# The last turns moved into their own slot, x^T's copies ahead of the weight conversion, and four weight pieces converted two slots later

## The chip, the core and the metric

The kernel runs on one NeuronCore of a Trainium2 chip. The time is that of one execution on the device, in microseconds (us). Five engines run their own instruction queues in order and meet at semaphores: PE (TensorE, the matmuls; its weight loads are listed apart as PEld), DVE (VectorE), ACT (ScalarE), POOL (GpSimd) and SP (SyncE, which only issues DMAs here). A number such as L401 is a line of the kernel before; where the kernel after is meant, its lines are some 1 to 18 further down.

## The reference

Attention with a threshold, and then a two-layer network with an exact GELU on the attention's output:

```python
scores = (1.0 / np.sqrt(64)) * np.matmul(q, k.transpose(0, 1, 3, 2))   # q, k, v: (8, 8, 576, 64)
thresh = np.max(scores, axis=-1, keepdims=True) - tau
scores = np.where(scores >= thresh, scores, -1e9)
scores = scores - np.max(scores, axis=-1, keepdims=True)
attn = np.exp(scores)
attn = attn / (np.sum(attn, axis=-1, keepdims=True) + 1e-09)
x = np.matmul(attn, v)           # then (B, H, S, D) -> (B*S, H*D): 4608 tokens x 512
h = x @ w_in                     # 512 -> 2048
g = 0.5 * h * (1.0 + erf(h / sqrt(2)))
out = g @ w_out                  # 2048 -> 512
```

The two weights arrive as float64 and have to be made float32 in the kernel; everything else is float32.

## The kernel before

**Slots.** The 64 heads are handled as 32 pairs `p` of heads, and the 576 queries of a pair in five chunks `i`: four of 128 (both heads, `e` = 0 and 1) and one of 64 + 64 (`i == NC`, both heads in one tile). One (p, i) is a slot `n`. One loop over `n` writes out, in program order, all that the engines do; nothing reorders it afterwards. The first batch element (pairs 0 to 3, the "early" pairs) has slots 0 to 19: slots 0 to 7 are chunks 0 and 1 of its pairs, slots 8 to 19 chunks 2, 3 and NC of each pair in turn, so that slot 19 is (3, NC). From slot 20 (`BATCH`) on the slots go pair by pair.

**A slot.** `scores` (PE, `sc`, L401) multiplies K^T and Q^T into two PSUM tiles, of which there are two in all, so the next slot's scores wait until this slot's are used up. `softmax_head`: DVE takes the negative row maximum (`nmx`, L413), POOL the threshold (`thr`, L416), ACT the exponential (`p`, L418). `softmax_tail`: DVE masks and sums (L434), which frees the score tile. For early pairs the probabilities are turned on PE one slot later (`turn_p_early`, `tr`, L347) and copied out of PSUM into `pT` by ACT (L354, L358, L363, L367). Slot 19's own turn is written out at the end of slot 20, and its copies are DVE's (`p == EARLY - 1`). From slot 20 on DVE turns the probabilities (L533) and SP regroups them by DMA. `weigh_v` multiplies V with the turned probabilities (PE, `xT`, L572) and ACT copies the result into the token block `xall` (L582). For an early pair's tokens from 256 on, that is put on a list (`due`) when its last turn is written out, and done in the next slot: slots 12, 15, 18 and 21.

**The network beside it.** `fill` puts matmuls of the two layers between the attention's: layer 1 `hT` (L664), whose results are kept as plain copies (L631) until slot 20, and layer 2 `o_ps` (L679), which needs them through the GELU. In slot 20 ACT switches its table, runs eight GELUs (L637) and switches back (L650). `fill` writes out a matmul only when the weight piece that it reads was written out before it as converted. `owed` is the work that fill may place in a slot; in slot 21 it places 0.4 of it and keeps the rest for slot 22.

**Conversion.** Each weight is loaded in 16 pieces of 128 x 512 float64, 32 in all, in this order: `w_in`, then `w_out` row block by row block, so that pieces 28 to 31 are blocks j = 12 to 15 of layer 2. A raw piece lies in a free slot of `xall` or in half of `turned_p`. Converting one takes four steps on three engines: `convert_first` on ACT (two activations, L199 and L200, into a `power` tile and the weight), `convert_second` on DVE (L207, L208), after which the next piece's load is issued by SP (L183), and `add_low_bits` on POOL (L219), the sum that finishes the piece. Of one slot's pieces the newest sum is written out ahead of the next slot's `thr`, the others behind both of its `thr`. The `power` tiles come from the pool `gp` of ten buffers, in which the GELU results lie too. `STEPS[n]` is the number of pieces that slot n converts, written out at the end of the slot; `convert_ahead` keeps one piece whose ACT part is done ahead. In slots 12, 15 and 18 (`hi == S` in `due`) the ACT part is written out ahead of `weigh_v` and its copies:

```python
        if early and n > START and any(hi == S for _, *_, hi in due):
            convert_ahead(STEPS[n] if n < BATCH - 1 else LATER)
```

`keep_busy` (L297) writes out matmuls on the identity whose result nobody reads; `BUSY` names the slots that have it. The rest of the kernel (the last ten token blocks, from L734 on) is not touched.

Of the kernel before, what the change touches and what calls it, by code (L numbers as in the profile page):

```python
# [9 lines left out]
U32 = mybir.dt.uint32  # L10
# [8 lines left out]
def kernel(  # L19
# [28 lines left out]
    nc = tc.nc  # L48
    ctx.enter_context(tc.manual_schedule())

    B, H, S, D = q.shape
    d_model, d_ff = moe_w_in.shape
    P = 128
    Q = 32
    HP = H // 2
    NP = B * HP
    EARLY = HP
# [44 lines left out]
    def x_slot(want=None):  # L102
        i = max(x_free) if want is None else want
        x_free.remove(i)
        return i
# [8 lines left out]
    def x_rows(i):  # L114
        return xall[:, i, :, :].rearrange("p c t -> p (c t)")
# [37 lines left out]
    pieces += [(w_out_sb[j][:, f:f + PIECE], moe_w_out[j * P:(j + 1) * P, f:f + PIECE])  # L153
               for j in range(N_DF) for f in range(0, d_model, PIECE)]
    wide = moe_w_in.dtype != FP32
    LATER = 2
    raws = []
    loaded = [0]
    converted = [0]

    def load_piece(eng=nc.sync):
        k = loaded[0]
        if k == len(pieces):
            return
        staged = k % 2 and k < len(pieces) - LATER
        if wide and not staged and not x_free:
            return
        dst, src = pieces[k]
        loaded[0] += 1
        if not wide:  # L170
            nc.sync.dma_start(dst, src)
            converted[0] += 1
            load_piece()
            return
        slot = []
        if staged:

            half, at = divmod(k // 2 % 4, 2)
            raw = pd[half].bitcast(U32)[:, at * 2 * PIECE:(at + 1) * 2 * PIECE]
        else:  # L180
            slot = [x_slot()]
            raw = x_rows(slot[0]).bitcast(U32)
        eng.dma_start(raw, src.bitcast(U32))  # L183
        raws.append((dst, raw, slot))

    ahead = []

# [34 lines left out]
    def convert_ahead(steps):  # L222

        while raws and len(ahead) <= steps:
            convert_first()

    def convert(steps):

        while steps > 0 and (ahead or raws):
            convert_ahead(1)  # L230
            convert_second()
            steps -= 1
# [104 lines left out]
    def turn_p_early(p, i):  # L337


        s = st[p]  # L340
        if i == 0 or (p < HP and i == 2):
            s["pT"] = [one.tile([P, KR, S], FP32, tag=f"pT{e}", name=f"pT{e}") for e in range(2)]
        w = s.pop(("p", i))
        n = 1 if i == NC else 2

        def turn(to, at):
            nc.tensor.transpose(to, w[:, at:at + P], ident)  # L347

        for e in range(n):
            tr = ps.tile([P, NC, P], FP32, tag="mm", name="tr")  # L350
            for c in range(NC):
                turn(tr[:, c, :], e * (S + TAIL) + c * P)
            if i < NC:
                nc.scalar.copy(s["pT"][e][:, 0:NC, i * P:(i + 1) * P], tr)  # L354
        if i == NC:
            copy = nc.vector.tensor_copy if p == EARLY - 1 else nc.scalar.copy
            for e in range(2):
                copy(s["pT"][e][:, 0:NC, MAIN:S], tr[:, :, e * TAIL:(e + 1) * TAIL])  # L358
        tails = s["pT"][0][:, NC, :]
        tr = ps.tile([P, NC, P], FP32, tag="mm", name="tr")  # L360
        turn(tr[:, 0, :], MAIN if i < NC else S - P)
        if i < NC:
            nc.scalar.copy(tails[:, i * P:(i + 1) * P], tr[:, 0, :])  # L363
            return
        for e in range(2):
            rows = slice(e * TAIL, (e + 1) * TAIL)
            copy(tails[rows, MAIN:S], tr[P - TAIL:P, 0, rows])  # L367

    def scale_q(p):
        t = st[p]["q"]  # L370
# [50 lines left out]
    def softmax_tail(p, i):  # L421

        s = st[p]
        sc, thr, w = s.pop(("sc", i)), s.pop(("thr", i)), s["p", i]
        n = len(sc)
        if p < EARLY and i < 2:
            pair = small.tile([P, 2], FP32, tag="den", name="den", bufs=2 * HP)
            den = [pair[:, e:e + 1] for e in range(n)]
        else:
            at = [e * NC + i if i < NC else 2 * NC for e in range(n)]  # L430
            den = [sums[p % 2][:, x:x + 1] for x in at]
        for e in range(n):
            row = w[:, e * S:(e + 1) * S].rearrange("p (h s) -> p h s", h=2)
            nc.vector.scalar_tensor_tensor(  # L434
                row, sc[e][:, :, 0:HALF], thr[:, e:e + 1], row, op0=ALU.is_ge, op1=ALU.mult, accum_out=den[e])
        if p < EARLY and i < 2:
            nc.gpsimd.tensor_scalar(pair[:, 0:n], pair[:, 0:n], 1e-9, None, op0=ALU.add)
            s["sum", i] = pair[:, 0:n]
        elif p < EARLY and i == NC:
            at = sums[p % 2][:, 0:2 * NC + 1]  # L440
            nc.gpsimd.tensor_scalar(at, at, 1e-9, None, op0=ALU.add)
# [112 lines left out]
            for e in (1, 0):  # L554
                nc.sync.dma_start(by_64(s["pT"][e])[:, 2 * a + h, :, :], turned_p[rows, e, h, :, :])

    def weigh_v(p, lo, hi):


        b, hp = divmod(p, HP)  # L560
        s = st[p]
        xT = ps.tile([P, 512], FP32, tag="mm", name="xT")
        for c in range(KR):
            for e in range(2):
                f = slice(e * D, (e + 1) * D)
                to = xT[f, 0:hi - lo]
                if p < EARLY:
                    rhs = s["pT"][0 if c == NC else e][:, c, lo:hi]
                else:
                    to = to.rearrange("p (g s) -> p g s", s=2 * Q)  # L570
                    rhs = by_64(s["pT"][e])[:, lo // (2 * Q):hi // (2 * Q), c, :]
                nc.tensor.matmul(  # L572
                    to, lhsT=s["v"][:, e, c, :], rhs=rhs, start=(c == 0), stop=(c == KR - 1))
        for n, o, at, size in in_blocks(b, lo, hi):
            if n not in x_blk:
                x_at[n] = x_slot(x_place(n))
                x_blk[n] = xall[:, x_at[n], :, :]
            to, x = x_blk[n][:, hp, o:o + size], xT[:, at - lo:at - lo + size]
            if p < EARLY and size == TOK:
                to = to.rearrange("q (p c) -> q c p", c=2)  # L580
                x = x.rearrange("q (c p) -> q c p", c=2)
            nc.scalar.copy(to, x)  # L582

    def weigh_half(p, c):

# [14 lines left out]
    def in_blocks(b, lo, hi):  # L600
        while lo < hi:
            n, o = divmod(b * S + lo, TOK)
            size = min(TOK - o, hi - lo)
            yield n, o, lo, size
            lo += size
# [513 lines left out]

    HALVED = (2, 3)  # L1120
    DIVIDE_LATE = {14: 0, 16: 1, 19: 2, 22: 3}
    STEPS = [0, 1, 1, 1, 1, 1, 2, 1, 2, 2, 2, 2, 3, 2, 2, 3, 2, 2, 2]
    BUSY = {1: 2, 6: 2, 8: 2, BATCH: 4}

    tokens = 0
    owed = 0.0
# [3 lines left out]
    for n in range(len(slots) + WEIGH + 1):  # L1130
# [17 lines left out]
        if n == BATCH:  # L1148
            gelus_held()
        table()  # L1150
        if early and n > START and any(hi == S for _, *_, hi in due):
            convert_ahead(STEPS[n] if n < BATCH - 1 else LATER)
        for args in due:
            if len(args) == 2:
                weigh_half(*args)
                if args[1]:
                    divide_early(args[0], 0, TOK)
                continue
            weigh_v(*args)
            if args[1] == 0:  # L1160
                divide_early(*args)
        due = []
        if n in DIVIDE_LATE:
            divide_late(DIVIDE_LATE[n])
        if p > EARLY and i == WEIGH:
# [10 lines left out]
            turn_p_early(*last)  # L1176
        if p < NP:
            softmax_tail(p, i)
        if p < NP and not early:
            turn_p(p, i)  # L1180
        if p < NP and not early:
            if i == 2:
                regroup(p, 1)
            if i > 2:
                regroup(p, i)
            if i == NC:
                divisors(p)
        if last and last[0] < EARLY and last[1] == NC:
            turn_p_early(*last)
        if p < 2 and i == 0:  # L1190
            for _ in range(2):
# [21 lines left out]
            scale_q(p + 1)  # L1213
        if p >= HP - 1 and i == 2 and p + 1 < NP:
            turn_qk(p + 1)
        convert(STEPS[n] if n < BATCH - 1 else len(pieces))
        if not early:
            lag[0] = 2 if p < NP else 0
            if n != BATCH:
                share = 0.4 if n == BATCH + 1 else 1.0  # L1220
                fill(owed * share, tokens)
                owed *= 1.0 - share
        if n in BUSY:
            keep_busy(BUSY[n])
        if last and last[0] < EARLY:
            if last[1] < 2 and last[0] in HALVED:
                due.append((last[0], last[1]))
            elif last[1] == 1:
                due.append((last[0], 0, TOK))
            if last[1] == NC:  # L1230
                due.append((last[0], TOK, S))
        if n == START - 1:
            tokens = TOK
        elif n == BATCH + 1:
            tokens = S
        elif p > EARLY and i == DIVIDE and p % HP == 0 or p == NP and i == WEIGH:
            tokens = p // HP * S
            leaving += [n for n in AWAY if n in x_blk and (n + 1) * TOK <= tokens]
        elif leaving and i < 2:
            put_away(leaving.pop(0))  # L1240
# [35 lines left out]
```

## Time and profile before

| what | value |
|---|---|
| median of three runs | 1333.94 us (1333.72 to 1334.61) |
| the profiled execution | 1333.98 us, of which its span 1332.1 us, 1.88 us around it |
| PE, DVE, ACT, POOL busy over the span | 99%, 78%, 45%, 48% |
| slots 0 to 19 | from 0 to 124.8 us; the scores of slot 20 start at 123.61 us |
| granted TensorE clock | 0.999 |

The profiler gives each instruction a start and a length. A row of the timeline merges equal instructions that follow each other: start, time from the first one's start to the last one's end, engine, line, operation, tiles, count, and in square brackets the idle time ahead of it with the instruction that ended the idle time. A float32 matmul counts as two records, so that x8 is four `sc` matmuls and x2 one of layer 2. The records of one engine overlap a little, so the step from start to start is what counts. A busy PE of 99% doesn't mean that PE never waits: a wait of a few tenths lies inside the records.

### The profile page before, as it was taken

How to read it: one execution, taken by the hardware profiler on the slowest of the kernel's cores; microseconds unless marked ns; L12 is line 12 of the kernel's file. 1: busy time of each engine (PE TensorE's matmuls, PEld its weight loads, DVE VectorE, ACT ScalarE, POOL GpSimd, SP SyncE). 2: the span in 40 equal slices, each digit the busy share in tenths (PEclk: the TensorE clock that was granted, in tenths of full speed). 3: DMA queues.
4: the chain of work that ended last, by engine and by line, in shares of the span. 5: the costliest groups of instructions: out<-in, count | busy, mean ns of one | idle time of the engine just before them, and what ended most of it. 6: DMA issues, size and time to landing. Idle time of an engine off the chain costs nothing.

```text
span 1332.1 us, 19898 instructions
## 1 busy us (share of the span) xinstructions
PE 1317.4 (99%) x6322; PEld 891.8 (67%) x6322; DVE 1041.0 (78%) x2003; ACT 603.8 (45%) x1025; POOL 635.2 (48%) x1058
## 2 busy tenths in 40 slices
PE   9999999999999999999999999999999999999998
PEld 6766466476476466466466556568788787877877
DVE  6887787788888888888888888783857698386674
ACT  7987357267367358348448438232211203211120
POOL 3555454545655655655655641236264403645530
PEclk9999999999999999999999999999999999999999
DMA  8463666776876887887797775400000130000003
GB/s 257 167 180 86 135 149 155 167 171 154 188 176 153 191 191 156 188 201 160 181 211 155 174 180 113 107 8 1 1 0 1 40 103 17 0 1 0 1 0 79
DMA packets 213687, 153.14 MB, mean 115 GB/s; under 512 B 117264, under 2 KB 196992, under 8 KB 213584
## 3 DMA queue, kind: packets, MB, share of 16 engines
q1 hardware_dynamic: 195440, 125.31, 40.6%
q0 software_dynamic: 17712, 26.26, 7.6%
q8 instruction: 52, 0.85, 0.3%
q14 instruction: 51, 0.42, 0.1%
q10 hardware_dynamic: 432, 0.30, 0.1%
HBM read 56.62 MB, written 12.58 MB: 52 GB/s over the span
## 4 chain that ended last, share of the span: by engine, by line
PE 91%; DVE 3%; ACT 2%; issue 1%; DMA 1%; POOL 1%; SPq 0%; DVEq 0%; POOLq 0%; ACTq 0%
PE bank L852 34%; PE o_ps L679 17%; PE hT L664 16%; PE sc L401 13%; PE xT L572 11%; DVE nmx L413 1%; DVE p L434 1%; ACT p L418 1%; PE tr L347 1%; DVE power L208 1%; DVE power L207 1%; ACT power L199 0%; DMA inv<-turned 0%; ACT w_out L200 0%; POOL thr L416 0%
## 5 line engine op out<-in xcount | busy, mean ns | idle before, releaser
L418 ACT ACTIVATE p<-sc,nmx 128x576 f32<-128x576 f32 x288 | 201.8, 737 | 282.3 <-DVE nmx L413 282.0
L434 DVE SCALAR_TENSOR_TENSOR p<-sc,thr,p 128x576 f32<-128x576 f32 x288 | 225.2, 815 | 72.9 <-ACT p L418 65.2
L416 POOL TENSOR_SCALAR thr<-nmx,tau_eff 128x1 f32<-128x1 f32 x288 | 83.9, 293 | 342.7 <-DVE nmx L413 340.8
L413 DVE TENSOR_REDUCE nmx<-sc 128x1 f32<-128x576 f32 x288 | 205.3, 749 | 46.9 <-PE sc L401 45.6
L664 PE MATMUL hT<-xall,w_in 128*128 128x256 f32 x1024 | 241.8, 386 | 0.0
L679 PE MATMUL o_ps<-w_out,g 128*128 128x512 f32 x512 | 236.8, 603 | 0.0
L664 PEld LDWEIGHTS hT<-xall,w_in 128*128 128x128 f32 x1024 | 189.4, 190 | 51.2 <-issue 24.5
L734 DVE TENSOR_TENSOR o<-o,bank 128x256 f32<-128x256 f32 (+1 forms) x242 | 99.9, 416 | 94.6 <-PE bank L852 89.6
L734 DVE TENSOR_TENSOR c<-c,bank 128x320 f32<-128x320 f32 x304 | 147.1, 487 | 33.8 <-PE bank L852 20.1
L679 PEld LDWEIGHTS o_ps<-w_out,g 128*128 128x128 f32 x512 | 93.1, 190 | 109.6 <-issue 106.5
L401 PE MATMUL sc<-kT,qT 64*128 64x288 f32 x960 | 159.8, 429 | 2.3 <-DVE p L434 1.6
L572 PE MATMUL xT<-pT,v 128*64 128x320 f32 (+1 forms) x1240 | 159.6, 409 | 0.7 <-DVE pT L358 0.5
L533 DVE STREAM_TRANSPOSE turned_p<-p 128x1152 f32<-128x1152 f32 x112 | 154.4, 1378 | 3.9
L401 PEld LDWEIGHTS sc<-kT,qT 64*128 64x128 f32 x960 | 91.4, 186 | 75.8 <-issue 60.4
L572 PEld LDWEIGHTS xT<-pT,v 128*64 128x64 f32 x1240 | 86.5, 137 | 71.5 <-issue 11.1
L852 PE MATMUL bank<-w_out,c 128*128 128x256 f32 (+1 forms) x484 | 120.5, 379 | 0.8 <-DVE o L734 0.8
L260 POOL DMA_DIRECT2D v<-in_v_dram x208 | 110.8, 536 | 3.7 <-issue 1.7
L852 PEld LDWEIGHTS bank<-w_out,c 128*128 128x128 f32 x484 | 90.3, 190 | 18.9 <-DVE o L734 3.2
L919 ACT ACTIVATE c<-c 128x320 f32<-128x320 f32 (+1 forms) x80 | 46.9, 624 | 114.6 <-DVE c L734 114.5
L852 PE MATMUL bank<-t_out,g 128*128 128x256 f32 (+1 forms) x324 | 82.4, 377 | 0.4 <-DVE o L734 0.4
L852 PE MATMUL bank<-t_out,c 128*128 128x256 f32 x320 | 82.8, 381 | 0.0
L734 POOL TENSOR_TENSOR c<-c,g 128x320 f32<-128x320 f32 (+1 forms) x40 | 50.5, 1271 | 67.5 <-DVE c L734 67.5
(186 smaller groups left out, 1753.7 us busy)
## 6 DMA issues: line engine op xcount, KB each, us to landing
pT<-turned_p SPq DMA_DIRECT2D x448, 160.0 KB, 3.6
pT<-pd_tail SPq DMA_DIRECT2D x112, 80.0 KB, 3.1
q<-in_q_dram POOLq DMA_DIRECT2D x104, 72.0 KB, 3.6
k<-in_k_dram POOLq DMA_DIRECT2D x104, 72.0 KB, 3.2
inv<-turned SPq DMA_DIRECT2D x54, 128.0 KB, 4.2
v<-in_v_dram POOLq DMA_DIRECT2D x156, 40.0 KB, 3.2
out_dram<-o SPq DMA_DIRECT2D x40, 128.0 KB, 2.4
xall<-in_moe_w_out_dram SPq DMA_DIRECT2D x9, 512.0 KB, 5.0
```

What stands on the lines that cost most here:

```text
L260: eng.dma_start(t[r:P:4, e, 0:n, :], rows[:, r * KR:r * KR + n, :])
L401: nc.tensor.matmul(sc[e][:, h, 0:HALF], lhsT=lhsT, rhs=s["kT"][rows, at:at + HALF], start=True, stop=True)
L413: nc.vector.tensor_reduce(nmx[:, e:e + 1], sc, axis=AXIS.XY, op=ALU.max, negate=True)
L416: nc.gpsimd.tensor_scalar(thr[:, e:e + 1], nmx[:, e:e + 1], -1.0, tau_eff, op0=ALU.mult, op1=ALU.subtract)
L418: nc.scalar.activation(w[:, e * S:(e + 1) * S].rearrange("p (h s) -> p h s", h=2), sc, AF.Exp, bias=nmx[:, e:e + 1], scale=1.0)
L434: nc.vector.scalar_tensor_tensor(row, sc[e][:, :, 0:HALF], thr[:, e:e + 1], row, op0=ALU.is_ge, op1=ALU.mult, accum_out=den[e])
L533: nc.vector.transpose(turned_p[:, :, i // 2, 0:NB, i % 2 * Q:(i % 2 + 1) * Q], w.rearrange("p (e b i) -> p e b i", e=2, i=Q))
L572: nc.tensor.matmul(to, lhsT=s["v"][:, e, c, :], rhs=rhs, start=(c == 0), stop=(c == KR - 1))
L664: nc.tensor.matmul(hT[:, j % 2, :], lhsT=w_in_sb[c][:, j * P:(j + 1) * P], rhs=x_blk[n][:, c, :], start=(c == 0), stop=(c == N_DM - 1))
L679: nc.tensor.matmul(o[:, 0:d_model], lhsT=g[j][:, m * P:(m + 1) * P], rhs=w_out_sb[j], start=(j == 0), stop=(j == N_DF - 1))
L734: eng.tensor_tensor(out, a, b, op=ALU.add)
L852: nc.tensor.matmul(to, lhsT=l, rhs=r, start=start and k == 0, stop=k == len(pairs) - 1, skip_group_check=not start)
```

## The change

- `LATER` is 4 in place of 2: raw pieces 28 to 31 are loaded into `xall`, none of them into `turned_p`. `load_piece` remembers a load that found no free slot (`wanted`) and issues it with a later one.
- `STEPS`: slots 2 and 4 convert no piece (one before), slots 6 and 18 one (two before), slots 21 and 22 two each (none before). Slot 18 leaves one piece with its ACT part done, so ACT does two pieces in slot 21 and one in slot 22.
- In slots 12, 15 and 18 the ACT part of the conversion is written out behind `weigh_v` and its copies.
- The turns of slot 19 are written out in slot 19, behind those of slot 18, and copied by ACT. Their `xT` comes in slot 20 (slot 21 before); its copies into `xall` are DVE's, behind slot 20's L533.
- `BUSY` loses its entry for slot 20: eight identity matmuls.
- In slot 21 `fill` places 0.75 of what is owed. In program order PE has eight layer-2 matmuls in slot 21 and three in slot 22, where it had four and seven; in slot 23 it has five (j = 11 to 15) both times.

```diff
-    LATER = 2
+    LATER = 4
...
     def load_piece(eng=nc.sync):
-        k = loaded[0]
-        if k == len(pieces):
-            return
-        staged = k % 2 and k < len(pieces) - LATER
-        if wide and not staged and not x_free:
-            return
...
+        wanted[0] += 1
+        while wanted[0] > 0 and loaded[0] < len(pieces):
+            k = loaded[0]
+            staged = k % 2 and k < len(pieces) - LATER
+            if wide and not staged and not x_free:
+                return
...
+            wanted[0] -= 1
...
         if i == NC:
-            copy = nc.vector.tensor_copy if p == EARLY - 1 else nc.scalar.copy
             for e in range(2):
-                copy(s["pT"][e][:, 0:NC, MAIN:S], tr[:, :, e * TAIL:(e + 1) * TAIL])
+                nc.scalar.copy(s["pT"][e][:, 0:NC, MAIN:S], tr[:, :, e * TAIL:(e + 1) * TAIL])
...
-    def weigh_v(p, lo, hi):
+    def weigh_v(p, lo, hi, copy=nc.scalar.copy):
...
+        if copy is None:
+            return xT
+        weighed(p, lo, hi, xT, copy)
+
+    def weighed(p, lo, hi, xT, copy):
...
-            nc.scalar.copy(to, x)
+            copy(to, x)
...
-    STEPS = [0, 1, 1, 1, 1, 1, 2, 1, 2, 2, 2, 2, 3, 2, 2, 3, 2, 2, 2]
-    BUSY = {1: 2, 6: 2, 8: 2, BATCH: 4}
+    STEPS = [0, 1, 0, 1, 0, 1, 1, 1, 2, 2, 2, 2, 3, 2, 2, 3, 2, 2, 1, 0, 0, 2, 2]
+    BUSY = {1: 2, 6: 2, 8: 2}
...
-        if early and n > START and any(hi == S for _, *_, hi in due):
-            convert_ahead(STEPS[n] if n < BATCH - 1 else LATER)
+        long = early and n > START and any(hi == S for _, *_, hi in due)
         for args in due:
...
+            if n == BATCH:
+                xT = weigh_v(*args, None)
+                continue
             weigh_v(*args)
...
+        if long:
+            convert_ahead(STEPS[n])
...
+        if n == BATCH - 1:
+            turn_p_early(p, i)
         if p < NP and not early:
             turn_p(p, i)
+        if n == BATCH:
+            weighed(EARLY - 1, TOK, S, xT, nc.vector.tensor_copy)
...
-        if last and last[0] < EARLY and last[1] == NC:
+        if last and last[0] < EARLY and last[1] == NC and early:
             turn_p_early(*last)
...
-        convert(STEPS[n] if n < BATCH - 1 else len(pieces))
+        convert(STEPS[n] if n < len(STEPS) else 0)
...
-                share = 0.4 if n == BATCH + 1 else 1.0
+                share = 0.75 if n == BATCH + 1 else 1.0
...
-            if last[1] == NC:
+            if last[1] == NC and early:
                 due.append((last[0], TOK, S))
+            if n == BATCH - 1:
+                due.append((p, TOK, S))
```

More of the change, by code (lines that the diff above doesn't have):

```diff
@@ L155 @@
     wide = moe_w_in.dtype != FP32
-    LATER = 2
+    LATER = 4
     raws = []
     loaded = [0]
+    wanted = [0]
     converted = [0]
     def load_piece(eng=nc.sync):
-        k = loaded[0]
-        if k == len(pieces):
-            return
-        staged = k % 2 and k < len(pieces) - LATER
-        if wide and not staged and not x_free:
-            return
[L168 to L184, printed above, removed]
+        wanted[0] += 1
[4 more added lines that the diff above has]
+                return
+            dst, src = pieces[k]
+            loaded[0] += 1
+            if not wide:
+                nc.sync.dma_start(dst, src)
+                converted[0] += 1
+                continue
+            wanted[0] -= 1
+            slot = []
+            if staged:
+                half, at = divmod(k // 2 % 4, 2)
+                raw = pd[half].bitcast(U32)[:, at * 2 * PIECE:(at + 1) * 2 * PIECE]
+            else:
+                slot = [x_slot()]
+                raw = x_rows(slot[0]).bitcast(U32)
+            eng.dma_start(raw, src.bitcast(U32))
+            raws.append((dst, raw, slot))
     ahead = []
@@ L366, in turn_p_early @@
             rows = slice(e * TAIL, (e + 1) * TAIL)
-            copy(tails[rows, MAIN:S], tr[P - TAIL:P, 0, rows])
+            nc.scalar.copy(tails[rows, MAIN:S], tr[P - TAIL:P, 0, rows])
     def scale_q(p):
@@ L573, in weigh_v @@
                     to, lhsT=s["v"][:, e, c, :], rhs=rhs, start=(c == 0), stop=(c == KR - 1))
+        if copy is None:
+            return xT
+        weighed(p, lo, hi, xT, copy)
+    def weighed(p, lo, hi, xT, copy):
+        b, hp = divmod(p, HP)
         for n, o, at, size in in_blocks(b, lo, hi):
@@ L1158 @@
                 continue
+            if n == BATCH:
+                xT = weigh_v(*args, None)
+                continue
             weigh_v(*args)
```

## The prediction

> **What bounds the kernel now.** I read the page first, then the chain of waits over the first 300 us, then each engine's timeline around the slots that are edited.
>
> ```profile
> PE 1317.4 (99%) x6322; PEld 891.8 (67%) x6322; DVE 1041.0 (78%) x2003; ACT 603.8 (45%) x1025; POOL 635.2 (48%) x1058
> PE 91%; DVE 3%; ACT 2%; issue 1%; DMA 1%; POOL 1%; SPq 0%; DVEq 0%; POOLq 0%; ACTq 0%
> ```
>
> PE bounds the whole, and what isn't PE on the chain lies at the start:
>
> ```profile
> 77.92 0.47 ACT xall L582 x2
> 78.44 0.81 PE tr L347 x5
> 79.24 0.99 PE sc L401 x4
> 80.25 0.77 DVE nmx L413
> ...
> 129.98 3.14 PE xT L572 x20
> 133.13 3.63 PE o_ps L679 x8
> 136.76 1.54 PE sc L401 x8
> 138.29 6.21 PE o_ps L679 x14
> ```
>
> Up to 130 us the chain goes to and fro between ACT, DVE and PE; from 130 us on it is PE without a hole. So what a slot before 20 saves or a slot after 20 loses shifts all that follows. PE's timeline shows the holes that the edits aim at:
>
> ```profile
> 78.44 0.81 PE L347 MATMUL tr<-ident,p 128*128 128x128 f32 x5 [0.72 <-ACT xall L582]
> ...
> 98.71 0.33 PE L347 MATMUL tr<-ident,p 128*128 128x128 f32 x1 [0.83 <-ACT xall L582]
> ...
> 118.31 0.82 PE L347 MATMUL tr<-ident,p 128*128 128x128 f32 x5 [0.88 <-ACT xall L582]
> ...
> 125.38 1.95 PE L297 MATMUL idle<-ident 128*128 128x128 f32 x16
> 127.52 1.94 PE L401 MATMUL sc<-kT,qT 64*128 64x288 f32 x8 [0.19 <-DVE p L434]
> 129.98 3.14 PE L572 MATMUL xT<-pT,v 128*64 128x320 f32 x20 [0.52 <-DVE pT L358]
> ```
>
> In slots 12, 15, 18 a turn waits for a PSUM buffer, which x^T's copy gives back only after ACT's conversions. In slot 20 PE idles on identity matmuls.
>
> **What the skill says.** (1) "PSUM — Partial Sum Buffer", Engine vs sequencer instructions: ACT, DVE and POOL are strict FIFO, matmuls start in program order. The trace agrees: no matmul passes the waiting turn at 118.31. A waiting matmul thus holds up everything behind it. (2) "TensorE: Matmul & The Clock Gate", part 1: after an idle window of about 3.4 us PE runs at half clock until some 3.4 us of work have passed. The trace shows the start: the first sixteen q records take 2.12 us (at 4.17), the next pair's sixteen 1.09 us (at 9.80). It shows no hole of 3 us later on. (3) "ScalarE: Activation LUTs", What ACT_TABLE_LOAD costs: 1283 ns a load; here 1.28 us, twice in slot 20.
>
> **The gain, slots 0 to 19.** Steps from start to start: L199 and L200 0.58 us each, so ACT gives 1.16 us to a piece; L207 and L208 0.46 + 0.61 = 1.07 us on DVE; L219 1.28 us on POOL.
>
> - Slots 2 and 4: nothing. The next slots' scores (22.55, 28.23, 33.06, 38.75) hang on the q/k turns, on ACT's pT copies and on PE's x^T, none of which is behind the two pieces; exponentials come 1 us earlier and then wait for PE.
> - Slot 6: DVE goes from L208 straight to slot 7's maximum at 45.27; without one piece that could start at 44.20, but scores start at 43.52 and take 1.27, so 44.79: 0.48 gained. Slot 7's mask waited 0.33 for `thr` behind L219 (47.09), whose place is now empty: 0.2 more. Its later L207 took 0.96 in place of 0.46 beside POOL work: another 0.2. Sum 0.9.
> - Slots 12, 15, 18: the copies now run where x^T is done, before the pieces. The waits 0.72, 0.83 and 0.88 go, and the score start behind them moves 0.84, 0.83, 1.02. DVE's pieces are over before the new maximum starts (78.4 against 79.4), so nothing is next. Sum 2.7.
>
> Gain 3.6 us at slot 19 (2.7 to 4.5: one slot's share may be eaten by raw loads, which take about 5 us to land; the removed load-ahead keeps the same number of pieces between load and use, so I take none). On SP the last piece's load now stands behind v's loads, about 122 us, and is used in slot 22, some 20 us later; the others move a few places with the pieces that trigger them: nothing.
>
> **Slots 19 to 24, on the clock of the kernel before (subtract 3.6).** Slot 19's turns now come at 123.75 (their buffers are freed by the pT copies of slot 18), so scores 20 start at 124.4, not 123.61, and four more ACT copies, 1.13 us, lie ahead of the exponentials of slot 20: 126.46 against 125.67. All of ACT's table and GELU block moves by 0.79: exponentials of slot 21 at 135.34.
>
> ```profile
> 127.57 1.28 ACT L637 ACT_TABLE_LOAD   x1
> 128.86 4.27 ACT L637 ACTIVATE g<-g 128x512 f32<-128x512 f32 x8
> 133.15 1.28 ACT L650 ACT_TABLE_LOAD   x1
> ...
> 134.55 1.35 ACT L418 ACTIVATE p<-sc,nmx 128x576 f32<-128x576 f32 x2
> ```
>
> PE uses the wait: x^T 125.6 to 128.5, scores 21 to 130.0, eight layer-2 matmuls (0.9 each) from the first GELU at 130.2 to 137.4, scores 22 to 138.7, three more to 141.4. The removed identity matmuls, 1.95 us, lay in this wait. DVE gives up the pT copies (1.2 us) and takes x^T's (0.6, from 130.2); its maximum of slot 21 is over at 132.1, well ahead of ACT's exponential at 135.34: nothing. At 138.7 PE is four matmuls ahead for 0.5 us more: 3.1 us ahead. Then the moved pieces come, and their order matters:
>
> - DVE: mask of slot 21 until 137.65, L533 until 139.03, two pieces until 141.17, only then the maximum of slot 22 (138.28 before).
> - ACT's second piece of slot 21 needs a `power` buffer. Of `gp`'s ten buffers eight hold GELU results until layer 2 has read them, so two are left, and in the program order it waits for POOL's L219 of the first one, which waits for DVE's L208 at 141.17: 142.5. The exponentials of slot 22 are queued behind it: 143.7 (not 141.9). Mask until 146.06; scores 23 need it: 145.3 to 147.0. PE, free since 141.4, is idle for **3.9 us**.
> - Layer 2, j = 11 to 13, until 149.7. j = 14 reads a piece of slot 22. DVE: L533 until 147.44, next pair's turns (L383 to L389) 149.18, two pieces 151.32. POOL: L219 of the newest piece 152.63, two `thr` (maximum of slot 23) 153.15, L219 of j = 14 154.4. PE waits **4.7 us** for it, and scores 24 are behind: j = 14, 15 until 156.3.
>
> Scores 24 start at 150.00 before:
>
> ```profile
> 138.22 6.28 PE L679 MATMUL o_ps<-w_out,g 128*128 128x512 f32 x14
> 144.43 1.24 PE L401 MATMUL sc<-kT,qT 64*128 64x288 f32 x8
> 145.60 4.56 PE L679 MATMUL o_ps<-w_out,g 128*128 128x512 f32 x10
> 150.00 1.13 PE L401 MATMUL sc<-kT,q_tail 128*128 128x288 f32 x4
> ```
>
> POOL's q, k and v loads (L251, L260) stand beside or behind the sums; they are for pairs one and two further on, so their delay of up to 4 us costs nothing. With the same matmuls done, the change stands 6.3 us later there. After slot 24 DVE and ACT are ahead again and PE keeps its rate.
>
> Sum: 6.3 - 3.6 = +2.7 us. The two holes pass the idle window of (2), and PE is two thirds idle from 141.4 to 154.4. A half clock after the first hole is hidden by the second; after the second it costs half of 3.4 to 6.8 us, 1.7 to 3.4 by the page. Whether the window falls so, no trace of before shows; below zero it can't be. I take a small part, +0.3, and keep the whole for the range. From 1333.98, the profiled execution's own time and 0.04 above the median, 1333.98 + 3.0 = **1337.0 us**.
>
> **Rivals.**
> - Clock: the half clock takes hold: 2.7 + 2.3 gives 1339. For it, two holes above 3.4 us, close together; against it, the window's phase is free.
> - No buffer wait: the power buffer comes free earlier, or the semaphore is met sooner. Scores 23 then start at 143.7, j = 14 at 152.8: 4.6 - 3.6 = +1.0, 1335. The kernel's program order speaks against it.
> - Faster, by the idle time taken up: DVE is idle 3.26 us ahead of slot 21's mask and ACT 6.05 us in slot 23. Were the moved pieces taken into such time and layer 2 not held up, the lead of 3.1 at slot 22 stays: 3.6 + 3.1 = 6.7, 1327.3. Against it: the pieces are written out behind the mask, not in DVE's idle time. The point that decides is the sum of the two holes, 8.6 us by my count: at 5.9 the change is even, below 3.2 it is faster by more than 0.2%.
> - The order is not what I think: the eight identity matmuls and the moved turns are plain in the instruction order, so no.
>
> **How the numbers follow.** The main case, +2.7 with 1 us to either side, has 0.42; clock 0.29; no buffer wait or a larger early gain 0.18; idle time taken up 0.11. A measurement of this kernel can tell about 0.2%, 2.7 us, from no change. Slower by more: 0.6 of the main case, all of the clock case, a little of the third: 0.56. Faster by more: the last case, 0.11. Within: 0.33. The range reaches from a part of the last case, with the gain at 4.5 and a short hole, 1332.5, to the clock case with a small gain, 1341.0.
>
> **What would show it.** Right: no ACT x^T wait ahead of turns in slots 12, 15, 18; scores 20 some 2.8 us earlier; a hole of about 4 us ahead of scores 23 with ACT's second L199 of slot 21 waiting for POOL; a hole of 4 to 5 us ahead of layer 2's j = 14, released by POOL L219; eight matmuls of layer 2 in slot 21 without waits. Half clock would show as o_ps records of 0.9 us in place of 0.45. Wrong: scores 24 earlier than 150.0 us, or maxima of slot 22 ahead of the pieces.

## Result and the profile after

The kernel after takes 1339.88 us (median of six runs, 1338.52 to 1340.22), the kernel before 1334.18 us (1332.53 to 1334.61): ratio 1.0043, 95% interval 1.0033 to 1.0053. That is 5.7 us slower, where 1337.0 was forecast. From here on, a line number without a kernel's name is one of the kernel after (there L348 is the turn, L355 the copy of a turned tile, L590 x^T's copy, L220 POOL's sum, L687 layer 2, L639 the copy ahead of the GELU). Shifts are starts of `sc` in the profiled executions, after minus before.

The page of the profile after, busy time and the chain's shares:

```profile
PE 1318.6 (99%) x6306; PEld 892.5 (67%) x6306; DVE 1039.8 (78%) x2001; ACT 604.9 (45%) x1027; POOL 635.5 (48%) x1058
PE 92%; ACT 3%; DVE 2%; issue 1%; DMA 1%; POOL 0%; SPq 0%; DVEq 0%; POOLq 0%; ACTq 0%
```

Nothing in it says where 5.6 us of span come from: PE is still 99% busy. The list of PE's waits does. First of the kernel before (waiting tile and line, releaser, us in total, times, longest):

```profile
PE tr L347 <- ACT xall L582: 2.4, 3, 0.9
PE sc L401 <- DVE p L434: 1.8, 7, 0.5
```

and then of the kernel after:

```profile
PE sc L401 <- DVE p L434: 5.7, 7, 3.7
PE tr L348 <- ACT pT L355: 2.2, 4, 0.9
PE o_ps L687 <- POOL w_out L220: 2.1, 1, 2.1
```

The waits for x^T's copy are gone, but waits for a copy of the turned probabilities stand in their place. Two new long ones have come, ahead of scores and ahead of a layer-2 matmul. PE's timeline of the kernel after has them in place:

```profile
77.84 0.33 PE L348 MATMUL tr<-ident,p 128*128 128x128 f32 x1 [0.79 <-ACT pT L355]
...
95.79 1.15 PE L348 MATMUL tr<-ident,p 128*128 128x128 f32 x9
...
116.77 0.33 PE L348 MATMUL tr<-ident,p 128*128 128x128 f32 x1 [0.91 <-ACT pT L355]
...
137.14 2.84 PE L687 MATMUL o_ps<-w_out,g 128*128 128x512 f32 x6
143.72 3.00 PE L401 MATMUL sc<-kT,qT 64*128 64x288 f32 x8 [3.74 <-DVE p L434]
146.65 4.09 PE L687 MATMUL o_ps<-w_out,g 128*128 128x512 f32 x6
152.83 1.99 PE L687 MATMUL o_ps<-w_out,g 128*128 128x512 f32 x4 [2.10 <-POOL w_out L220]
154.65 1.13 PE L401 MATMUL sc<-kT,q_tail 128*128 128x288 f32 x4
```

The first three rows are the turns of slots 12, 15 and 18: only slot 15 lost its wait. The others are slots 22 and 23: a hole of 3.7 us ahead of scores 23, then six records of layer 2 that take 4.1 us where six took 2.8 before the hole, then a hole of 2.1 us ahead of j = 14. Scores 24 start at 154.65, in the kernel before at 150.00.

What ended the first hole is seen on ACT, in the kernel after:

```profile
135.38 0.66 ACT L200 ACTIVATE power<-xall 128x512 f32<-128x512 f32 x1
...
140.81 0.66 ACT L200 ACTIVATE power<-xall 128x512 f32<-128x512 f32 x1 [4.19 <-POOL w_out L220]
...
141.93 1.35 ACT L418 ACTIVATE p<-sc,nmx 128x576 f32<-128x576 f32 x2
```

and on DVE:

```profile
137.61 0.69 DVE L209 SCALAR_TENSOR_TENSOR power<-xall,power 128x512 uint32<-128x512 uint32 x1
...
139.28 1.42 DVE L413 TENSOR_REDUCE nmx<-sc 128x1 f32<-128x576 f32 x2
142.75 0.82 DVE L434 SCALAR_TENSOR_TENSOR p<-sc,thr,p 128x576 f32<-128x576 f32 x1 [2.05 <-ACT p L418]
```

As forecast, slot 22's maximum (139.28) stands behind the two late pieces, and the exponentials (141.93) behind an ACT piece that waits for a `power` buffer. What ended the second hole is seen on POOL:

```profile
149.73 1.26 POOL L220 TENSOR_TENSOR w_out<-power,w_out 128x512 uint32<-128x512 uint32 x1 [3.55 <-DVE power L209]
150.98 0.57 POOL L416 TENSOR_SCALAR thr<-nmx,tau_eff 128x1 f32<-128x1 f32 x2
151.52 1.26 POOL L220 TENSOR_TENSOR w_out<-power,w_out 128x512 uint32<-128x512 uint32 x1
```

The first sum is that of j = 15, the newest piece, which is written out first; the sum of j = 14, which PE waits for, is the second one, behind both `thr`. The granted clock in four stretches around the holes (us, length, then busy time of PE, PEld, DVE, ACT, POOL, then PEclk, DMA share, GB/s):

```profile
138.94:142.36 3.42, 1.04 (x3) 0.19 (x1) 1.76 (x3) 1.55 (x3) 2.84 (x4) 1.00 0.91 166
142.36:145.77 3.41, 2.05 (x7) 1.69 (x8) 2.99 (x6) 2.03 (x4) 3.41 (x7) 0.50 0.87 224
145.77:149.18 3.41, 3.41 (x6) 1.29 (x5) 3.31 (x8) 0.00 (x0) 0.41 (x1) 0.50 0.30 76
149.18:152.60 3.42, 1.55 (x4) 0.38 (x2) 3.02 (x6) 1.41 (x2) 2.87 (x4) 1.00 0.00 0
```

From about 142.4 to 149.2 us PE ran at half clock.

The shifts add up as follows. The profiled run of the kernel after begins 0.47 us ahead (full clock came earlier; over all profiled kernels this start varies by 1.24 us). Slots 0 to 19 gain 1.56 (shift -2.03 at scores 19), the moved turns cost 0.94 (scores 20), slots 20 to 24 cost 5.74 (scores 24 at +4.65), and 0.95 more comes in small steps up to the end of the span (+5.6).

### The profile page after: what moved, and what is told of

Read it like the earlier page. It is cut to its first block, busy times and chain, and to the rows that moved or that the text cites. A ratio compares the mean times of both kernels' runs of the same rounds, so it can differ in the third digit from the quotient of the medians.

```text
span 1337.7 us, 19863 instructions
## 1 busy us (share of the span) xinstructions
PE 1318.6 (99%) x6306; PEld 892.5 (67%) x6306; DVE 1039.8 (78%) x2001; ACT 604.9 (45%) x1027; POOL 635.5 (48%) x1058
## 4 chain that ended last, share of the span: by engine, by line
PE 92%; ACT 3%; DVE 2%; issue 1%; DMA 1%; POOL 0%; SPq 0%; DVEq 0%; POOLq 0%; ACTq 0%
PE bank L860 34%; PE hT L672 16%; PE o_ps L687 16%; PE sc L401 13%; PE xT L572 11%; ACT p L418 1%; PE tr L348 1%; DVE nmx L413 1%; DVE p L434 0%; DVE power L209 0%; DVE power L208 0%; ACT pT L355 0%; DMA xall<-in_moe_w_out_dram 0%; ACT power L200 0%; PE xT L604 0%
## 5 line engine op out<-in xcount | busy, mean ns | idle before, releaser
L687 PE MATMUL o_ps<-w_out,g 128*128 128x512 f32 x512 | 238.3, 606 | 2.3 <-POOL w_out L220 2.1
L687 PEld LDWEIGHTS o_ps<-w_out,g 128*128 128x128 f32 x512 | 93.7, 191 | 113.1 <-issue 108.1
L533 DVE STREAM_TRANSPOSE turned_p<-p 128x1152 f32<-128x1152 f32 x112 | 154.4, 1378 | 3.9
```

What stands on the lines that cost most here:

```text
L533: nc.vector.transpose(turned_p[:, :, i // 2, 0:NB, i % 2 * Q:(i % 2 + 1) * Q], w.rearrange("p (e b i) -> p e b i", e=2, i=Q))
L687: nc.tensor.matmul(o[:, 0:d_model], lhsT=g[j][:, m * P:(m + 1) * P], rhs=w_out_sb[j], start=(j == 0), stop=(j == N_DF - 1))
```

## Experiments

Three questions: which part of the change makes the holes; what each hole costs, with its half clock and buffer wait; and where the early gain went.

**1. The pieces put back.** The kernel after with

```diff
-    LATER = 4
+    LATER = 2
-    STEPS = [0, 1, 0, 1, 0, 1, 1, 1, 2, 2, 2, 2, 3, 2, 2, 3, 2, 2, 1, 0, 0, 2, 2]
+    STEPS = [0, 1, 1, 1, 1, 1, 2, 1, 2, 2, 2, 2, 3, 2, 2, 3, 2, 2, 2]
```

> The changed kernel with STEPS and LATER as they were before; the moved turns, the conversions behind x^T's copies, the removed identity matmuls and the share of 0.75 stay. Theory (the four late pieces make both holes): no hole of over 1 us ahead of scores 23 and of layer 2's j = 14; the lead of about 3 us that layer 2 builds in slots 20 and 21 stays, slot 15's 1.0 us too, while slot 6's 1.0 us goes; together about 4 us below the kernel before, 1330 us (ratio to before 0.997). Rival (the moved turns and x^T's late copies make the holes by themselves): the holes stay, 1338 to 1341 us (ratio 1.003 to 1.005).

Measured: 1331.64 us against 1333.60, ratio 0.9985 (0.9979 to 0.9992), faster than both kernels. PE's timeline has no hole:

```profile
138.28 2.84 PE L687 MATMUL o_ps<-w_out,g 128*128 128x512 f32 x6
141.06 1.79 PE L401 MATMUL sc<-kT,qT 64*128 64x288 f32 x8
142.78 4.56 PE L687 MATMUL o_ps<-w_out,g 128*128 128x512 f32 x10
147.18 1.21 PE L401 MATMUL sc<-kT,q_tail 128*128 128x288 f32 x4
```

Scores 24 stand 2.82 us earlier than in the kernel before, with scores 20 at +0.06 (slot 15's gain and the moved turns cancel): so the lead that layer 2 builds in slots 20 to 22 is real, 2.9 us. Of it 0.7 is lost again by scores 26, the time keeps 2.0. The theory holds; its size, 4 us, was twice what came.

**2. The pieces alone.** The kernel before with the new `STEPS`, `LATER`, loader and `convert(STEPS[n] if n < len(STEPS) else 0)`; `convert_ahead(STEPS[n])` comes to the same as before in slots 12, 15 and 18. All else is as before (`sc` is L402 and layer 2 L680 here).

> The kernel before with the moved pieces alone: STEPS, LATER, the loader and the end of the conversion as in the changed kernel, all else as before, the identity matmuls of slot 20 too. Theory (pieces make the holes): two holes again, ahead of scores 23 and of layer 2's j = 14, 1338 to 1341 us (ratio to before 1.003 to 1.005), a little above the changed kernel, for slot 15's 1.0 us is missing. Rival (moved turns make them): within 1 us of the kernel before, 1333 to 1335 us.

Measured: 1340.40 us, ratio 1.0049 (1.0037 to 1.0062). PE's timeline:

```profile
143.79 1.94 PE L402 MATMUL sc<-kT,qT 64*128 64x288 f32 x8 [0.33 <-DVE p L435]
145.67 2.84 PE L680 MATMUL o_ps<-w_out,g 128*128 128x512 f32 x6
152.89 3.60 PE L680 MATMUL o_ps<-w_out,g 128*128 128x512 f32 x4 [4.38 <-POOL w_out L220]
```

Theory right on the time. But there is one hole, not two: with the old share, seven matmuls of layer 2 lie in slot 22, and PE does there what it would wait for; the whole wait then stands ahead of j = 14. Experiments 1 and 2 together: the moved pieces make the loss, the moved turns and the later ACT conversions do not.

**3. Two late pieces in place of four.**

```diff
-    STEPS = [0, 1, 0, 1, 0, 1, 1, 1, 2, 2, 2, 2, 3, 2, 2, 3, 2, 2, 1, 0, 0, 2, 2]
+    STEPS = [0, 1, 1, 1, 1, 1, 1, 1, 2, 2, 2, 2, 3, 2, 2, 3, 2, 2, 1, 0, 0, 1, 1]
```

> The changed kernel with two pieces late in place of four, one each in slots 21 and 22; slots 2 and 4 have their piece back, slot 6 still has one fewer. Theory (each slot's first late piece is nearly covered, the second is what PE waits for: a piece costs some 1.1 us on DVE and 1.2 to 1.3 us on ACT and POOL, against a lead of about 3 us, and the wait for a power buffer needs a second piece in the slot): holes of about 1 us each in place of 3.7 and 2.1, slot 6's gain stays and slots 2 and 4 show nothing; 1332 to 1334 us (ratio to before 0.998 to 1.000). Rival (cost goes with the number of pieces): half of the changed kernel's loss in slots 20 to 24, 2.9 of 5.7 us, so 1337 us (ratio 1.002). If slots 2 and 4 mattered, scores 5 and 6 would start later than in the changed kernel by more than 0.3 us.

Measured: 1333.39 us, ratio 0.9996 (0.9988 to 1.0004), the theory's value. PE's timeline, where the two holes are now short:

```profile
140.46 1.94 PE L401 MATMUL sc<-kT,qT 64*128 64x288 f32 x8 [1.04 <-DVE p L434]
142.33 3.70 PE L687 MATMUL o_ps<-w_out,g 128*128 128x512 f32 x8
146.72 1.13 PE L687 MATMUL o_ps<-w_out,g 128*128 128x512 f32 x2 [0.68 <-POOL w_out L220]
```

From scores 20 to 24 this kernel gains 0.4 us on the kernel before (-1.64 to -2.04), where experiment 1 gains 2.9 and the kernel after loses 5.7: the first two late pieces cost 2.5 us, the other two 6.1 more. Slots 2 and 4 give nothing, as predicted, but leaving them empty costs something later: with a piece in each, scores 11 and 12 stand at the same shift (-1.65, -1.66); in the kernel after they go from -1.47 to -1.10. There the second tile of scores 11 waits 0.48 us for slot 10's mask, and that for `thr` behind POOL's L220, which started 0.35 us later. All six profiled kernels with slots 2 and 4 empty show this step, none of the others. Why L220 starts later is open.

**4. Identity matmuls in the first hole.** `BUSY` of the kernel after gets `BATCH + 2: 14`.

> The changed kernel with 28 more identity matmuls at the end of slot 22, ahead of scores 23, where PE is idle for 3.7 us (they fill about 3.4 us at the 122 ns that the sixteen of slot 20 took each). Theory (the half clock of about 142 to 149 us is hidden by the hole ahead of layer 2's j = 14): clock at full speed there, layer 2's six matmuls behind scores 23 take 2.7 us in place of 4.1, the hole behind them grows from 2.1 to about 3.5 us, and the time stays within 0.5 us of the changed kernel, 1339.5 us (ratio to before 1.004). Rival (half clock costs time): 1.4 to 3 us less, 1337 to 1338 us (ratio 1.002).

Measured: 1341.01 us, ratio 1.0052 (1.0039 to 1.0065): no faster than the kernel after, and by the intervals not told from it; in the traces its scores 24 come 1.5 us later. The size was wrong: I had taken 16 records for 16 matmuls, so that the filling was twice the hole, 6.4 us, and scores 23 came 2.3 us late. Even so, j = 14 started at 152.72, where it starts at 152.83 in the kernel after: the second hole took up the delay. Half clock then came behind that hole, and its four records took 3.58 us for 1.99.

**5. Both holes filled**, with the size put right: `BUSY` gets `BATCH + 2: 7`, and `block_steps` calls `keep_busy(10)` ahead of the first block's j = 14.

> The changed kernel with both of PE's holes filled by identity matmuls: 14 of them (28 records, 3.2 us) ahead of scores 23, 20 (40 records, 4.6 us) ahead of layer 2's j = 14. With 28 of them in the first hole alone, twice what fits, scores 23 came 2.3 us late, but j = 14 only 0.1 us earlier than in the changed kernel, and its four records then ran at half clock. Theory (the half clock of 142 to 149 us is hidden by the second hole): full clock from 136 to 156 us, j = 14 starts where it did (152.8) and scores 24 too (154.65); within 0.5 us of the changed kernel, 1339.5 us (ratio 1.0043). Rival (half clock costs time, by the second hole or later): 1 to 3 us less, 1337 to 1338.5 us.

Measured: 1339.82 us, ratio 1.0046 (1.0032 to 1.0059). PE's timeline (layer 2 is L689 here):

```profile
139.70 3.29 PE L298 MATMUL idle<-ident 128*128 128x128 f32 x28
143.65 1.94 PE L401 MATMUL sc<-kT,qT 64*128 64x288 f32 x8 [0.66 <-DVE p L434]
145.52 2.84 PE L689 MATMUL o_ps<-w_out,g 128*128 128x512 f32 x6
148.20 4.63 PE L298 MATMUL idle<-ident 128*128 128x128 f32 x40
152.77 1.98 PE L689 MATMUL o_ps<-w_out,g 128*128 128x512 f32 x4
154.59 1.13 PE L401 MATMUL sc<-kT,q_tail 128*128 128x288 f32 x4
```

The clock is full all through, and scores 24 start within 0.06 us of where they do in the kernel after: its half clock cost nothing, the second hole hid it. The chain on DVE, ACT and POOL sets both ends. In that chain one order was not tried. DVE was done with j = 14's piece at 148.52 and POOL was idle until 149.73, but j = 14's sum began at 151.52. An estimate from these times: written out first, that sum would be ready at about 149.8, before PE has done j = 13 (146.65 + 4.09 = 150.74), and most of the second hole would go. No run shows it.

**6. The buffer wait, first try.** The `power` tiles of all four late pieces from the pool `op` (two buffers):

```diff
-        power = gp.tile([P, PIECE], U32, tag="g", name="power")
+        begun[0] += 1
+        pool, tag = (op, "o_sb") if begun[0] > len(pieces) - LATER else (gp, "g")
+        power = pool.tile([P, PIECE], U32, tag=tag, name="power")
```

> The changed kernel, with the power buffers of its four late pieces taken from pool op (tag o_sb, same size, two buffers, free at that time) in place of gp, so that none of them waits for a buffer that GELU results keep short. Theory (ACT's second piece of slot 21 waits 4.2 us for POOL's L220, and the exponentials of slot 22 behind it are late by more than the maximum makes them): no wait of ACT's L200 for POOL, exponentials of slot 22 start at their maximum, at 140.0; scores 23 about 1.7 us earlier, and the DVE and POOL work behind them as well, so layer 2's j = 14 too; 1338 us (ratio to before 1.0030). Rival (the exponentials wait for the maximum, which stands behind the pieces on DVE, all the same; the buffer costs nothing): within 0.5 us of the changed kernel, 1339.5 us (ratio 1.0043).

Measured: 1339.09 us, ratio 1.0039 (1.0026 to 1.0052). It decides nothing: with four pieces in two buffers ACT waits for the first of POOL's sums again, as ACT's timeline shows:

```profile
140.65 0.66 ACT L203 ACTIVATE power<-xall 128x512 f32<-128x512 f32 x1 [4.20 <-POOL w_out L223]
```

**7. The buffer wait, second try.** The same with `- 2` in place of `- LATER`, so that two pieces use gp's two free buffers and two op's.

> The changed kernel with the power buffers of its last two pieces alone taken from pool op. With all four from op's two buffers the third piece again waited 4.2 us for L220 of the first (so that run decided nothing); now two pieces have gp's two free buffers and the last two have op's. Theory (the buffer wait holds up the exponentials of slot 22): ACT's second L200 of slot 21 waits for nothing on POOL, the exponentials start at their maximum near 140.1 in place of 141.9, the mask near 141.05 (bound by thr on POOL) in place of 142.75, scores 23 and all behind them 1.7 us earlier: 1338.2 us (ratio to before 1.0033). Rival (the wait is replaced in full by that for the maximum and thr): within 0.5 us of the changed kernel, 1339.5 us (ratio 1.0043).

Measured: 1339.12 us, ratio 1.0039 (1.0027 to 1.0052). ACT's timeline (exponentials are L421, pieces L203 and L204):

```profile
137.04 0.66 ACT L203 ACTIVATE power<-xall 128x512 f32<-128x512 f32 x1
...
140.59 1.41 ACT L421 ACTIVATE p<-sc,nmx 128x576 f32<-128x576 f32 x2 [2.33 <-DVE nmx L416]
```

and PE's:

```profile
142.60 2.79 PE L404 MATMUL sc<-kT,qT 64*128 64x288 f32 x8 [2.09 <-DVE p L437]
...
153.53 1.13 PE L404 MATMUL sc<-kT,q_tail 128*128 128x288 f32 x4
```

The wait is gone, the exponentials follow their maximum, and scores 20 to 24 take 30.47 us in place of 32.13: 1.66 us, as the theory has it. The median moved by 0.8 us alone, and the intervals of the two kernels overlap; how much of the 1.66 stays in the time these runs don't tell.

**8. The pT copies first.** Experiment 1's kernel, with `convert_ahead(STEPS[n])` of slots 12, 15 and 18 put behind `turn_p_early(*last)`.

> STEPS and LATER as before, the rest of the changed kernel, and in slots 12, 15 and 18 the conversions of ACT stand not only behind x^T's copies but also behind the copies of the turned probabilities (L355, L363). Theory (in slots 12 and 18 PE's wait for x^T's copy was replaced by one for L355, which stood behind the pieces): the waits of 0.79 and 0.91 us ahead of a turn go, slots 12 and 18 give what slot 15 gave; 1.5 us less than with the pieces put back and ACT's order left (1331.6 us), so 1330 us (ratio to before 0.9973). Rival (ACT then ends its pieces later, DVE's L209 behind them too, and the next slot's maximum stands behind that on DVE): the time saved on PE is lost again at the maximum, within 0.4 us of 1331.6 us (ratio 0.9985).

Measured: 1337.55 us, ratio 1.0023 (1.0016 to 1.0029): 5.9 us slower than experiment 1. Its 21 runs spread from 1334.19 to 1339.04, and the profiled one is near the low end, so the trace shows the kind of loss and not all of it. PE's timeline:

```profile
77.29 0.33 PE L348 MATMUL tr<-ident,p 128*128 128x128 f32 x1 [0.29 <-ACT pT L355]
...
82.79 0.82 PE L348 MATMUL tr<-ident,p 128*128 128x128 f32 x5 [1.17 <-ACT g L639]
...
89.48 1.94 PE L401 MATMUL sc<-pd_tail,qT 64*128 64x288 f32 x8 [1.37 <-DVE p L434]
```

The wait in slot 12 did shrink, from 0.78 to 0.29 us; what came after took more. ACT stands idle for 2.8 us ahead of the copies and then does its three pieces from 77.82 to 81.3 (before the copies, 74.88 to 78.4, in experiment 1; that trace starts 1.2 us later than this one, so the real delays are that much longer than times side by side show). DVE, in the same trace:

```profile
78.52 0.43 DVE L208 TENSOR_SCALAR power<-power 128x512 uint32<-128x512 uint32 x1 [3.32 <-ACT power L200]
...
82.54 0.82 DVE L434 SCALAR_TENSOR_TENSOR p<-sc,thr,p 128x576 f32<-128x576 f32 x1 [1.05 <-POOL thr L416]
```

Its pieces wait 3.3 us for ACT, the next maximum follows at 80.74 (80.30 in experiment 1), the mask then waits for POOL, and ACT's later copies (L639) hold up PE's buffers. The rival is right, and worse than it was put.

**9. One piece in slot 6, the last one in slot 19.** The kernel after with `LATER = 2` and

```diff
-    STEPS = [0, 1, 0, 1, 0, 1, 1, 1, 2, 2, 2, 2, 3, 2, 2, 3, 2, 2, 1, 0, 0, 2, 2]
+    STEPS = [0, 1, 1, 1, 1, 1, 1, 1, 2, 2, 2, 2, 3, 2, 2, 3, 2, 2, 2, 1]
```

> The changed kernel with LATER = 2 and the old STEPS but for one piece: slot 6 has one, not two, and slot 19 takes the last one; nothing in slots 20 to 22. Theory (slot 6's second piece is what cost 1.0 us in slots 6 to 9, and slot 19 has room before the GELU block): no holes in slots 22 and 23, scores 9 about 1.0 us earlier than in the kernel before; 0.6 to 1.0 us less than with the pieces put back whole (1331.6 us), so 1330.6 to 1331 us (ratio to before 0.9978). Rival (slot 19's piece delays the exponentials of slot 20 and with them all GELUs and layer 2 by up to 1.2 us): 1331.5 to 1333 us (ratio 0.9985 or more).

Measured: 1333.18 us, ratio 0.9997 (0.9989 to 1.0006). Slot 6's gain is there (scores 9 gain 0.95 on scores 0), but `convert_ahead(2)` in slot 18 now found two pieces to start, not one, ahead of the copies that PE waits for:

```profile
117.82 0.33 PE L348 MATMUL tr<-ident,p 128*128 128x128 f32 x1 [2.03 <-ACT pT L355]
...
118.95 4.44 PE L672 MATMUL hT<-xall,w_in 128*128 128x256 f32 x12
```

Behind the hole of 2.0 us layer 1's twelve records took 4.4 us, with the clock at half:

```profile
120.00:122.00 2.00, 2.00 (x6) 1.64 (x5) 1.21 (x3) 1.16 (x2) 1.99 (x3) 0.50 0.14 33
```

**10. The same, with that conversion held back**: in slot 18 `convert_ahead(1)` in place of `convert_ahead(STEPS[n])`.

> As with one piece in slot 19 and one in slot 6, LATER = 2, but slot 18 starts one conversion on ACT ahead of the copies of the turned probabilities, not two: that second one made PE wait 2.0 us ahead of a turn, after which the records of layer 1 in slot 19 took 4.4 us for 2.75. Theory (slot 6's gain of 1.0 us is real and slot 19 has room): the wait in slot 18 is back at 0.9 us, scores 20 stand 1.0 us earlier than with the pieces put back whole, 1330.6 us (ratio to before 0.9977). Rival (the piece in slot 19 delays the exponentials of slot 20 and all GELUs behind): 1331.6 us or more (ratio 0.9985 or more).

Measured: 1331.18 us, ratio 0.9982 (0.9974 to 0.9989), the lowest of all, though not to be told from experiment 1's. From its own start, scores 20 stand 0.92 us earlier than in the kernel before, in experiment 1 none: slot 6's 1.0 us is kept. Of it little reaches the end. By scores 26 this kernel is 4.1 us ahead of the one before (1.0 of it from the earlier start), at scores 92 2.5: it loses 1.6 us on the way, in one wait of 0.6 us for a mask and steps without a wait in the trace.

**11. Experiments 8 and 9 together.**

> The last two together: slot 6 with one piece and slot 19 with the last one, and ACT's conversions in slots 12, 15 and 18 behind the copies of the turned probabilities. Theory: the gains add, 1.0 and 1.5 us below 1331.6 us, so 1329.1 us (ratio to before 0.9966), the fastest of all. Rival (each is eaten by DVE's or ACT's queue): 1331 us or more (ratio 0.998).

Measured: 1336.29 us, ratio 1.0018 (1.0011 to 1.0025), again with a wide spread (1334.12 to 1337.84). The rival's side, as after experiment 8; of the two parts it is that one's loss.

**12. The identity matmuls of slot 20 taken away**, in the kernel before (`BATCH: 4` out of `BUSY`).

> The kernel before without the eight identity matmuls of slot 20, nothing else. Theory (they lie in a wait of PE for slot 20's exponentials): scores 21 start at 127.5 as before, time within 0.7 us of the kernel before, 1333.7 us (ratio 0.9995 to 1.0005). Rival (they delay scores 21, which start 0.15 us after their end): up to 2 us faster. Second rival (they keep the clock): a hole of some 2.6 us there and half clock behind it, 1 to 3 us slower.

Measured: 1334.51 us, ratio 1.0005 (0.9997 to 1.0013), no difference that can be told. Scores 21 don't start earlier (shift -0.63, its start -0.73), so they lay in a wait. But they did something. PE's timeline without them:

```profile
126.89 2.14 PE L401 MATMUL sc<-kT,qT 64*128 64x288 f32 x8 [1.98 <-DVE p L434]
129.34 4.28 PE L572 MATMUL xT<-pT,v 128*64 128x320 f32 x20 [0.32 <-DVE pT L358]
```

x^T took 4.28 us for 3.14: half clock again, after a hole of 2.0 us. Scores 22 come 1.1 us later by it; slack ahead of scores 23 takes 0.4 of that back.

## Why the prediction was right or wrong

The range held the time and the sign was right; the likeliest value was 2.9 us too low. That the range held was in part luck: the main case with its 1 us to either side doesn't reach the time, and the upper end came from the clock case, whose cost was nothing. Step by step, in us of the profiled executions:

| step | predicted | measured |
|---|---|---|
| slots 2 and 4 | 0 | +0.37 (at slot 11) |
| slot 6 | -0.9 | -1.0 |
| slots 12, 15, 18 | -0.84, -0.83, -1.02 | 0, -1.04, 0 |
| moved turns, scores 20 | +0.8 | +0.94 |
| slots 20 to 24 | +5.5 | +5.74 |
| half clock | +0.3 | 0 |
| start, and after slot 24 | 0 | -0.47, +0.95 |
| sum | +3.0 | +5.6 |

The measured rows leave out 0.1 us of small steps in slots 12 to 18.

- **The failed step is the gain of slots 12 and 18, 1.9 us; measured: none.** "The waits 0.72, 0.83 and 0.88 go": x^T's wait did go. In these two slots it stood ahead of the fifth of a slot's nine turns, and the ninth turn waits for another buffer, the one that the first pT copy (L354 before, L355 after) gives back. With x^T's copy out of the way, that second wait ended last, 0.79 and 0.91 us, about as long as the first had been. It was there in the kernel before:

```profile
78.28 0.58 ACT L354 COPY pT<-tr 128x512 f32<-128x512 f32 x1
```

The copy ended at 78.86, and scores 13, right behind the ninth turn, started at 79.08. That turn takes about 0.17 us (77.84 to 78.01 in the kernel after), so less than 0.1 us was to be had. And the copy comes no earlier in the new order: ACT has the same work ahead of it, x^T's copies and the pieces, only turned round. Experiment 1, which starts level with the kernel before, has scores 13 at 79.13. In slot 15 the turn that waited for x^T's copy was the ninth itself, no turn waited for L355, and the slot gave its full share. The prediction looked for what is late next among DVE's pieces ("so nothing is next") and not among the turns' other buffers. Experiment 8 moved ACT's pieces once more, behind the pT copies: the wait in slot 12 shrank, and DVE, which needs the pieces, lost more.

- **Slots 2 and 4** gave nothing, as said; that they cost 0.37 us later was not foreseen.
- **Slots 20 to 24 were right in size and in their chain.** Scores 23 waited 3.7 us (3.9 said). The second hole measured 2.1 for 4.7, but scores 23 took 3.00 us where they take 1.94 at full clock (experiment 5) and six layer-2 records 4.09 for 2.84: 2.1 + 1.1 + 1.25 = 4.4. With the clock kept full, 4.6 us of identity matmuls fit in.
- **Clock**: that rival's 1339 is nearest to the measured time, but for another reason. Half clock took hold as it says, and experiment 5 shows that it cost nothing.
- **No buffer wait**: the wait was there. Its price, 1.8 us between 143.7 and 141.9, is 1.66 in the trace of experiment 7.
- **Idle time taken up** (1327.3): its assumption, no holes and a lead of 3.1 kept, is what experiment 1 makes true by leaving the pieces early. The lead measured 2.9, and 1331.6 was reached: slot 6's gain is missing there, slots 12 and 18 gave nothing, and part of the lead is lost again.
- **The removed identity matmuls lay in the wait**: right in the kernel before (experiment 12). In the kernel after and in experiment 1, PE works through that stretch and its clock stays full.

What stays open: the steps of 0.3 to 0.5 us behind slot 24 (0.95 in all in the kernel after, at about slots 81, 91 and 128), which no wait in the trace ends; the later L220 in slot 11; and what another order of POOL's sums would give.

## What to carry to other kernels

When an edit takes away the wait that ends last, look up everything else that the waiting instruction and the ones right behind it wait for, and put next to each the time at which it would be met: the second-latest is the gain's limit, and here it hung on the same queue as the first, so that turning the order round gave nothing. Work that is postponed to fill a quiet stretch has to be counted against the lead of the engine that will need its result: two late pieces used up nearly all of a lead of 3 us, four cost 5.7 us beyond it. And an order in one queue serves several consumers; putting one ahead (x^T's copy, then the pT copies) only helps while the next one behind still has slack.

## What the runs showed of the hardware

The Trainium skill, "TensorE: Matmul & The Clock Gate", part 1, has half clock come after at least one idle window of about 3.4 us. Here holes of 2.0 us did (experiments 9 and 12: twelve layer-1 records in 4.44 us for 2.75, x^T in 4.28 for 3.14), and after the first hole of the kernel after, 3.7 us long, half clock began 2.4 us into it and lasted 6.8 us. A hole of 2.1 us ahead of j = 14 in the same trace brought none: its four records took 1.99 us, against 3.58 behind one of 2.7 us in experiment 4. So the length of a hole alone does not tell whether half clock follows. Where it falls matters too, as the page's free-running window has it: between two changes of the granted clock lie whole multiples of 3.41 us in the traces (the kernel after: full for 136.53, half for 6.83, full for 1187.8; experiment 4: 146.77, 3.41 and 1181.0; experiment 12: 122.88, 3.41 and 1198.1). The four stretches shown under the result are such windows. The first had PE idle for 2.4 us, and half clock followed; the last, with most of the second hole, for 1.9 us, and none did. Over all traces no window at full clock with less than 1.5 us of idle time was followed by half clock, and every one with more than 2.0 was; between these it went both ways. So by these runs the idle window of the page need not be idle throughout. Eight identity matmuls in a wait, which did not change when scores 21 started, were enough to avoid it in slot 20.
